# Empty PSUM banks in the tensor engine's order: a NoSync chain on ScalarE and VectorE in a four-layer attention kernel

## The chip, the cores and the metric

The kernel runs on one core of a Trainium2 chip. The core has five engines with an instruction queue each: the tensor engine (PE in the profile, its weight loads PEld), VectorE (DVE), ScalarE (ACT), GpSimd (POOL) and SyncE (SP), which here only starts transfers. The metric is device time in microseconds (us), the median of several runs.

## The reference

Four layers in the order A, B, A, B on x of 2048 x 640 in fp32, each with a layernorm ahead and a residual after: 32 heads of 20. A is linear attention, B is infini attention: causal softmax inside each of four segments of 512 rows, mixed through a gate with a read from a memory that has collected the segments before.

```python
phi = lambda t: jnp.where(t > 0, t + 1, jnp.exp(t))
# A
kv = einsum("bhsd,bhse->bhde", phi(k), v); z = einsum("bhsd->bhd", phi(k))
o = einsum("bhqd,bhde->bhqe", phi(q), kv) / (einsum("bhqd,bhd->bhq", phi(q), z) + 1e-6)
# B, per segment s of 512
a_dot = softmax(qs @ ks.T * scale + causal_mask) @ vs
a_mem = (phi(qs) @ M) / (phi(qs) @ z + 1e-6)
o = g * a_mem + (1 - g) * a_dot
M = M + phi(ks).T @ vs;  z = z + sum(phi(ks))
```

## The kernel before

Products of fp32 matrices are made of two halves in f16 (a high part and the rest), three matmuls for each product. The dense part takes 128 rows or 320 or 512 columns at a time: L325 projects into rows of 320, L311 into a transposed 512, and both leave their result in a bank. PSUM has eight banks of 128 x 512 fp32. Every result of PE goes through one pool of eight, `bank()`; which of the eight a tile gets is settled at build time by the scheduler, from when it expects each to be free.

The program is written as two streams, `dense` (layernorms, transposes, projections, phi, memory, output projections) and `attend` (the softmax attention). `run` alternates between them by a modelled cost, and the order in which it issues matmuls is PE's order as it stands (`MANUAL = ("PE",)`). The order on DVE, ACT, POOL and SP is left to a scheduler, which places an instruction where it expects its inputs.

The attention goes in 64 groups of four heads (eight groups for each of four segments, in two B layers). A group's work is spread over three slots of three stretches (`STRETCHES`):

- row maxes: PE makes scores into two banks (L687, `ks,qs` or `qs,ks`), DVE adds the mask and reduces each with L694, which shows as two rows, the reduction and the read of its accumulator. L703 and L704 split the collected maxes into f16, PE turns them (L712), ACT copies them out (L714), and a transfer puts them as rows under the queries.
- exps: PE makes the scores again, now with the max subtracted (L729), ACT takes the exp out of the bank (L733), POOL sets what the mask hides to zero (L740).
- sums: PE multiplies by the values (L756), ACT copies the bank out (L762).
- normalise: PE turns that (L769), DVE takes the reciprocal of the sums (L772), the gate (L773) and the product out of the bank (L781, or L778 in segment 0), POOL adds to the output (L782).

Beside it the dense stream empties banks too: L272 on ACT copies the high half of a transpose (L268) and L273 on DVE subtracts it to get the rest; phi takes exp (L337) and relu (L339) of a projection; L348 copies the values; L391 adds the residual on DVE; L546 and L547 split queries and keys. A layernorm runs through DVE (L286, L288, L290), POOL (L291), DVE (L293) and ACT (L298).

Of the kernel before, what the change touches and what calls it, by code (L numbers as in the profile page):

```python
# [14 lines left out]
OP = mybir.AluOpType  # L15
# [109 lines left out]
class Kernel:  # L125
    def __init__(self, ctx, tc, A, const, out):
        self.ctx, self.tc, self.nc = ctx, tc, tc.nc
        self.A, self.const, self.out = A, const, out
        pool = lambda name, **k: ctx.enter_context(tc.tile_pool(name=name, bufs=1, **k))
        self.cp = pool("const")  # L130
        self.sb = pool("main")
        self.ps = pool("psum", space=PSUM)
        self.dr = pool("dram", space=DRAM)
        self.rate = 1.0
        self.q_pq, self.q_x, self.q_nat, self.q_row, self.q_w, self.q_pqi = [getattr(self.nc, e) for e in QUEUES]

    def bank(self):
        return self.ps.tile([P, 512], F32, tag="ps", name="ps", bufs=8)
# [122 lines left out]
    def turn(self, src, dst, i):  # L261

        nc = self.nc
        for c0, c1 in ((0, 3), (3, 5)):
            pt = self.bank()
            n = c1 - c0
            for c in range(c0, c1):
                nc.tensor.transpose(pt[:, (c - c0) * P:(c - c0 + 1) * P], src[:, c * P:(c + 1) * P],  # L268
                                    self.ident)
# [63 lines left out]
    def phi(self, p, inv, dst, eps):  # L333
        nc, sb = self.nc, self.sb
        n = p.shape[-1]
        e = sb.tile([P, 512], F32, tag="er", name="e", bufs=3)[:, :n]
        nc.scalar.activation(e, p, AF.Exp, scale=inv)  # L337
        r = sb.tile([P, 512], F32, tag="er", name="r", bufs=3)[:, :n]
        nc.scalar.activation(r, p, AF.Relu, scale=inv)  # L339
        if eps:  # L340
            nc.gpsimd.tensor_scalar(e, e, 1.0, eps, op0=OP.min, op1=OP.add)  # L341
            nc.vector.tensor_tensor(dst, e, r, op=OP.add)
        else:
            nc.vector.scalar_tensor_tensor(dst, e, 1.0, r, op0=OP.min, op1=OP.add)

    def v_half(self, p, v, n):
        vv = v[:, :H * E1].rearrange("p (h e) -> p h e", e=E1)
        self.nc.scalar.activation(vv[:, n * HB:(n + 1) * HB, :DH],  # L348
                                  p.rearrange("p (h e) -> p h e", e=DH), AF.Copy, scale=V_SHIFT)

    def new_v(self, user):

# [6 lines left out]
    def read_mem(self, pq, mem, dst, mul=None):  # L359

        nc, sb = self.nc, self.sb
        cut = HB * E1
        for k in range(2):
            nd = self.bank()
            cost, first = 0, True
            for t in range(C):
                a, b = LO[t] * E1, LO[t] * E1 + WID[t]
                lo, hi = max(a, k * cut), min(b, (k + 1) * cut)
                if lo < hi:
                    nc.tensor.matmul(nd[:, lo - k * cut:hi - k * cut], pq[t],  # L370
                                     mem[:, OFF[t] + lo - a:OFF[t] + hi - a],
                                     start=first, stop=True, skip_group_check=True)
# [4 lines left out]
            nc.vector.tensor_scalar(rc, nd[:, :, DH], 1e-6, None, op0=OP.add)  # L377
            nc.vector.reciprocal(rc, rc)
            if mul is not None:
                nc.vector.tensor_tensor(rc, rc, mul[:, k * HB:(k + 1) * HB], op=OP.mult)  # L380
            nc.vector.tensor_tensor(dst[:, k * HN:(k + 1) * HN].rearrange("p (h e) -> p h e", e=DH),
                                    nd[:, :, :DH], rc[:, :, None].to_broadcast([P, HB, DH]),
                                    op=OP.mult)
            yield cost

    def new_oT(self):
# [1 line left out]

    def o_half(self, oT, wo, L, x, xn, n):
        p = self.proj_n(oT, wo, 0, n)  # L390
        self.nc.vector.scalar_tensor_tensor(xn[:, n * HN:(n + 1) * HN], p, self.io[L],  # L391
                                            x[:, n * HN:(n + 1) * HN], op0=OP.mult, op1=OP.add)


    def norms(self, src, s, box, then=None):
# [21 lines left out]
    def a_first(self, s, xT, w, L, behind=None):  # L417
# [28 lines left out]
        def memory():  # L446
            for b0, b1 in ((0, 3), (3, 5)):
                p = self.bank()
                for i in range(NT):
                    for u in range(b0, b1):  # L450
                        a = OFF[u] - OFF[b0]
                        nc.tensor.matmul(p[:, a:a + WID[u]], pk[i][:, u * P:(u + 1) * P],  # L452
                                         v[i][:, LO[u] * E1:LO[u] * E1 + WID[u]],
                                         start=i == 0 and u == b0, stop=i == NT - 1,
                                         skip_group_check=True)
                a, b = OFF[b0], OFF[b1 - 1] + WID[b1 - 1]
                if s == 0:
                    nc.vector.tensor_copy(acc[:, a:b], p[:, :b - a])
                else:
                    nc.vector.tensor_tensor(acc[:, a:b], p[:, :b - a], acc[:, a:b], op=OP.add)  # L460
                yield (b - a) * 16 * COL
            if s == NSEG - 1:
                L["mem"] = self.masked(acc)
# [78 lines left out]
    def split_store(self, p, dd, t, key):  # L542

        nc = self.nc
        nat = self.bp.tile([P, 2, SEG], F16, tag="nat", name="nat", bufs=2)
        nc.scalar.activation(nat[:, 0], p, AF.Copy, scale=QK_SHIFT)  # L546
# [9 lines left out]
    def b_project(self, st):  # L556
# [14 lines left out]
        def pk_turn():  # L571
# [1 line left out]
            for i in range(NT):  # L573
                nc.tensor.transpose(pt[:, i * P:(i + 1) * P], pkT[:, i * P:(i + 1) * P], self.ident)  # L574
            pk = bp.tile([P, SEG], F32, tag="pkt", name="pkt", bufs=1)
            nc.scalar.activation(pk, pt, AF.Copy)
            return pk

        def update(t, pk):
# [4 lines left out]
                                 start=i == 0, stop=i == NT - 1)  # L584
            a = acc[:, OFF[t]:OFF[t] + WID[t]]
            if s == 0:
                nc.vector.tensor_copy(a, pm[:, :WID[t]])
            else:
                nc.vector.tensor_tensor(a, pm[:, :WID[t]], a, op=OP.add)

        for t in range(C):
            p = yield from self.proj_t(xT, w["q"], t)
# [85 lines left out]
    def row_max(self, G, todo):  # L678
# [11 lines left out]
        for par in range(2):  # L690
            for p, i, a in todo:
                n = (i + 1) * P
                junk = bp.tile([P, SEG], BF16, tag="junk", name="junk", bufs=1)
                nc.vector.tensor_tensor_reduce(junk[:, :n], bs[par][:, a:a + n], self.maskw[:, SEG - n:],  # L694
                                               1.0, NEG, OP.add, OP.max, G["mg"][:, par, p, i:i + 1])
        return cost

    def split_max(self, G):
# [5 lines left out]
        nc.vector.scalar_tensor_tensor(m2[:, :, 1], mg, -1.0 / M_ONE, m2[:, :, 0],  # L704
                                       op0=OP.mult, op1=OP.subtract)
        G["m2"] = m2

    def max_rows(self, G):
# [2 lines left out]
        pt = self.ps.tile([P, 1024], F16, tag="ps", name="pm", bufs=8)  # L711
        nc.tensor.transpose(pt[:32, :P], m2.rearrange("q a k r -> q (a k r)"), self.ident16)  # L712
        mt = bp.tile([32, P], F16, tag="mt", name="mt", bufs=2)
        nc.scalar.activation(mt, pt[:32, :P], AF.Copy)  # L714
# [5 lines left out]
    def scores(self, G, todo):  # L720
# [12 lines left out]
        nc.scalar.activation(e, b, AF.Exp, scale=self.lsc)  # L733
        starts = [a for _, _, _, a in todo]
        if len(starts) == 1:
            d, pat = e[:, :P], [[1, P]]
# [22 lines left out]

    def evacuate(self, G):  # L760
        G["oT"] = self.bp.tile([P, 512], F32, tag="oTf", name="oTf", bufs=1)
        self.nc.scalar.activation(G["oT"], G["pv"], AF.Copy)  # L762

    def normalize(self, G):
        nc, bp, sb, g, st = self.nc, self.bp, self.sb, G["g"], G["st"]
# [2 lines left out]
        for i in range(NT):  # L768
            nc.tensor.transpose(pt[:, i * P:(i + 1) * P], oT[:, i * P:(i + 1) * P], self.ident)  # L769
        pr = pt.rearrange("q (i h e) -> q i h e", i=NT, h=4)  # L770
        rc = sb.tile([P, NT, 4], F32, tag="rc4", name="rc4", bufs=2)
        nc.vector.reciprocal(rc, pr[:, :, :, DH])  # L772
        nc.vector.tensor_tensor(rc, rc, self.gate1[:, None, 4 * g:4 * g + 4].to_broadcast([P, NT, 4]),  # L773
                                op=OP.mult)
        o = st["o"][:, :, 80 * g:80 * g + 80].rearrange("q i (h e) -> q i h e", h=4)
        rb = rc[:, :, :, None].to_broadcast([P, NT, 4, DH])
        if st["s"] == 0:
            nc.vector.tensor_tensor(o, pr[:, :, :, :DH], rb, op=OP.mult)  # L778
        else:
            tmp = sb.tile([P, NT, 4, DH], F32, tag="er", name="tmp", bufs=3)  # L780
            nc.vector.tensor_tensor(tmp, pr[:, :, :, :DH], rb, op=OP.mult)  # L781
# [233 lines left out]
```

## Time and profile before

| | |
|---|---|
| median of three runs | 1830.06 us (1828.65 to 1834.99) |
| profiled execution | 1833.06 us |
| its span | 1831.3 us |
| PE busy | 1713.7 us, 94% |
| DVE busy | 1145.0 us, 63% |
| ACT busy | 911.1 us, 50% |
| POOL busy | 502.5 us, 27% |
| granted PE clock | 0.995 |

A row of a timeline gives the start in the span, the duration, the engine, the line, the operation, output<-inputs, the shape, the count of instructions of one kind drawn together, and in brackets the idle time ahead of it with what ended that. The rows of waits give, for all such idle times of a kind, the sum in us, the count and the mean. A wait for several things is put down to the one that came last.

### The profile page before, as it was taken

The numbers are of one execution on the slowest core, as the hardware profiler recorded it, in microseconds if no ns is written. First come the engines' busy times: TensorE is split into PE (matmuls) and PEld (weight loads), VectorE is DVE, ScalarE is ACT, GpSimd is POOL, SyncE is SP. The second block draws the span as 40 slices with busy tenths as digits, with TensorE's granted clock in tenths as the row PEclk, the third lists the DMA queues.
The fourth block names the chain that finished last, engine by engine and source line by source line (L and its number), as shares of the span: only waits on it lengthen the run. The fifth ranks groups of instructions, "written<-read, shape, count | busy, mean of one in ns | idle before, by whom it ended". The sixth has DMA issues, their size and how long they took to land.

```text
span 1831.3 us, 36161 instructions
## 1 busy us (share of the span) xinstructions
PE 1713.7 (94%) x13032; PEld 1070.3 (58%) x13032; DVE 1145.0 (63%) x3890; ACT 911.1 (50%) x1696; POOL 502.5 (27%) x925
## 2 busy tenths in 40 slices
PE   6999999999999999898989999999999989998998
PEld 4666676654664565453556776766546546544555
DVE  7655343677777676766663421527687777777783
ACT  5455433256556545545554433333664665565553
POOL 1534440022122113224344334200221231232231
PEclk9999999999999999999999999999999999999999
DMA  7452443312222332352212112432122222323332
GB/s 254 154 188 92 159 143 99 107 58 93 88 67 86 105 103 76 105 186 71 66 56 87 51 33 91 137 108 99 51 91 92 86 90 91 101 77 100 122 112 87
DMA packets 123307, 185.96 MB, mean 102 GB/s; under 512 B 13676, under 2 KB 85484, under 8 KB 120952
## 3 DMA queue, kind: packets, MB, share of 16 engines
q1 hardware_dynamic: 109416, 137.44, 23.5%
q0 software_dynamic: 4496, 25.23, 3.8%
q10 hardware_dynamic: 9216, 20.98, 3.0%
q8 instruction: 103, 1.69, 0.4%
q14 instruction: 76, 0.62, 0.1%
HBM read 104.41 MB, written 78.64 MB: 100 GB/s over the span
## 4 chain that ended last, share of the span: by engine, by line
PE 75%; DVE 11%; ACT 6%; issue 4%; POOL 2%; DMA 2%; SPq 1%; POOLq 0%; ACTq 0%; DVEq 0%
PE ps L325 33%; PE ps L311 18%; PE ps L756 7%; DVE junk L694 4%; PE ps L268 4%; ACT pe L733 3%; PE ps L370 3%; PE ps L729 3%; PE ps L452 2%; PE ps L687 2%; POOL e L341 1%; PE ps L582 1%; PE ps L769 1%; DVE nat L547 1%; PE ps L574 1%
## 5 line engine op out<-in xcount | busy, mean ns | idle before, releaser
L694 DVE CUSTOM_DVE_ANT_0 junk<-ps,maskw 128x512 bf16<-128x512 f32 (+3 forms) x1024 | 499.5, 488 | 83.2 <-PE ps L687 27.1
L733 ACT ACTIVATE pe<-ps,lsc 128x512 f32<-128x512 f32 x640 | 392.7, 691 | 174.5 <-PE ps L729 171.5
L740 POOL TENSOR_SCALAR_AFFINE_SELECT pe<-pe 128x256 f32<-128x256 f32 (+1 forms) x640 | 233.5, 371 | 677.4 <-ACT pe L733 672.0
L325 PEld LDWEIGHTS <-xT 128*128 128x128 f16 x2880 | 281.7, 99 | 124.1 <-issue 18.6
L325 PEld LDWEIGHTS <-oT 128*128 128x128 f16 x1920 | 187.1, 98 | 79.6 <-issue 7.6
L341 POOL TENSOR_SCALAR e<-e 128x320 f32<-128x320 f32 (+1 forms) x104 | 163.7, 1574 | 163.2 <-ACT e L337 154.4
L756 PE MATMUL ps<-pe,v 128*32 128x512 f32 (+3 forms) x2048 | 155.4, 438 | 13.7 <-ACT pe L733 6.8
L729 PE MATMUL ps<-qs,ks 62*128 62x384 f16 (+3 forms) x1024 | 132.2, 299 | 33.4 <-DVE mg L694 22.4
L325 PE MATMUL ps<-w_Bo,oT 128*128 128x320 f16 x960 | 142.8, 301 | 2.6 <-DVE mg L694 1.4
L325 PE MATMUL ps<-w_Bv,xT 128*128 128x320 f16 x960 | 141.3, 301 | 1.9 <-DVE mg L694 1.9
L325 PE MATMUL ps<-w_Av,xT 128*128 128x320 f16 x960 | 141.2, 305 | 1.6 <-DVE w_Av L234 1.0
L311 PE MATMUL ps<-xT,w_Bq 128*128 128x512 f16 x600 | 139.5, 379 | 1.5 <-DVE mg L694 0.9
L311 PE MATMUL ps<-xT,w_Bk 128*128 128x512 f16 x600 | 139.5, 379 | 0.2 <-DVE xn L391 0.2
L325 PE MATMUL ps<-w_Ao,oT 128*128 128x320 f16 x960 | 139.5, 299 | 0.0
L311 PE MATMUL ps<-xT,w_Aq 128*128 128x512 f16 x600 | 136.0, 379 | 1.3 <-DVE xT L273 0.9
L325 PE MATMUL ps<-w_Ak,xT 128*128 128x320 f16 x960 | 135.6, 299 | 1.4 <-DVE mg L694 1.4
L348 ACT ACTIVATE v<-ps 128x320 f32<-128x320 f32 x128 | 55.4, 436 | 143.2 <-PE ps L325 138.9
L291 POOL TENSOR_TENSOR rs<-rs,mhalf 128x1 f32<-128x1 f32 x64 | 35.3, 551 | 302.6 <-DVE rs L290 302.6
L687 PE MATMUL ps<-ks,qs 60*128 60x512 f16 (+3 forms) x1024 | 108.4, 297 | 5.8 <-ACT pe L733 3.6
L756 PEld LDWEIGHTS ps<-pe,v 128*32 128x32 f32 x2048 | 65.3, 110 | 81.2 <-issue 66.3
L547 DVE SCALAR_TENSOR_TENSOR nat<-ps,nat 128x512 f16<-128x512 f32 x80 | 55.3, 691 | 90.3 <-ACT nat L546 86.4
L546 ACT ACTIVATE nat<-ps 128x512 f16<-128x512 f32 x80 | 48.0, 600 | 105.9 <-PE ps L311 76.3
(151 smaller groups left out, 2240.9 us busy)
## 6 DMA issues: line engine op xcount, KB each, us to landing
x<-xn ACTq DMA_DIRECT2D x48, 320.0 KB
qs<-qd SPq DMA_DIRECT2D x128, 120.0 KB
ks<-kd SPq DMA_DIRECT2D x128, 120.0 KB
xo<-x SPq DMA_DIRECT2D x48, 320.0 KB
pqd<-pq POOLq DMA_DIRECT2D x40, 256.0 KB, 2.5
pqi<-pqd SPq DMA_DIRECT2D x32, 320.0 KB
qd<-nat SPq DMA_DIRECT2D x40, 256.0 KB
kd<-nat SPq DMA_DIRECT2D x40, 256.0 KB
```

Of the source, the lines that this page charges most:

```text
L268: nc.tensor.transpose(pt[:, (c - c0) * P:(c - c0 + 1) * P], src[:, c * P:(c + 1) * P], self.ident)
L311: nc.tensor.matmul(p, w[:, c, a, t * P:(t + 1) * P], xT[:, c, b, :], start=k == 0, stop=k == 3 * C - 1)
L325: nc.tensor.matmul(p, xT[:, c, a, i * P:(i + 1) * P], w[:, c, b, n * HN:(n + 1) * HN], start=k == 0, stop=k == 3 * C - 1)
L341: nc.gpsimd.tensor_scalar(e, e, 1.0, eps, op0=OP.min, op1=OP.add)
L348: self.nc.scalar.activation(vv[:, n * HB:(n + 1) * HB, :DH], p.rearrange("p (h e) -> p h e", e=DH), AF.Copy, scale=V_SHIFT)
L547: nc.vector.scalar_tensor_tensor(nat[:, 1], p, QK_SHIFT, nat[:, 0], op0=OP.mult, op1=OP.subtract)
L687: nc.tensor.matmul(bs[par][:, a:a + n], qs[r, p, i * P:(i + 1) * P], ks[r, p, :n], start=True, stop=True)
L694: nc.vector.tensor_tensor_reduce(junk[:, :n], bs[par][:, a:a + n], self.maskw[:, SEG - n:], 1.0, NEG, OP.add, OP.max, G["mg"][:, par, p, i ...
L729: nc.tensor.matmul(b[:, a:a + n], ks[r, p, j * P:(j + 1) * P], qs[r, p, j * P:], start=True, stop=True)
L733: nc.scalar.activation(e, b, AF.Exp, scale=self.lsc)
L740: nc.gpsimd.affine_select(d, d, pattern=pat, compare_op=OP.is_ge, fill=0.0, base=0, channel_multiplier=-1)
L756: nc.tensor.matmul(G["pv"][32 * h4:32 * h4 + 32, j * P:], v[j][:, h * E1:h * E1 + 32], G.pop((p, par, j)), start=j == 0, stop=j == 2, skip ...
```

## The change

Every instruction on ACT and DVE that is the first to empty a bank, and the two that split the maxes, goes through a new `seq`. It ties the instruction to the one that went through `seq` before it on the same engine, by a dependency without a semaphore: nothing waits at run time for it, but the scheduler may no longer swap the two. Since the program is written in PE's order, the tied instructions of an engine now issue in the order in which PE fills their banks. Instructions that aren't tied (L273, L547, the layernorm's, all on POOL and SP) are still placed by the scheduler, between the tied ones.

The tied lines are L272, L337, L339, L348, L546, L576, L714, L733, L762 on ACT, and L377 to L381, L391, L458, L460, L587, L589, L694, L703, L704, L772, L773, L778, L781 on DVE. The core of the diff; the other lines are wrapped in the same way:

```diff
+        self.last = {}
+    def seq(self, ins):
+        i = ins.ins
+        prev = self.last.get(i.engine)
+        if prev is not None:
+            self.tc.add_manual_dep(i, prev.name, mybir.DependencyInfo(mybir.DependencyClass.NoSync,
+                                                                      mybir.DependencyReason.DATA), reason="seq")
+        self.last[i.engine] = i
...
-            nc.scalar.activation(hi, v, AF.Copy)
+            self.seq(nc.scalar.activation(hi, v, AF.Copy))
             nc.vector.tensor_tensor(dst[:, c0:c1, 1, i * P:(i + 1) * P], v, hi, op=OP.subtract)
...
-        nc.scalar.activation(e, p, AF.Exp, scale=inv)
+        self.seq(nc.scalar.activation(e, p, AF.Exp, scale=inv))
...
-        nc.scalar.activation(r, p, AF.Relu, scale=inv)
+        self.seq(nc.scalar.activation(r, p, AF.Relu, scale=inv))
...
-                nc.vector.tensor_tensor_reduce(junk[:, :n], bs[par][:, a:a + n], self.maskw[:, SEG - n:],
-                                               1.0, NEG, OP.add, OP.max, G["mg"][:, par, p, i:i + 1])
+                self.seq(nc.vector.tensor_tensor_reduce(junk[:, :n], bs[par][:, a:a + n], self.maskw[:, SEG - n:],
+                                                        1.0, NEG, OP.add, OP.max, G["mg"][:, par, p, i:i + 1]))
...
-        nc.vector.tensor_scalar(m2[:, :, 0], mg, -1.0 / M_ONE, None, op0=OP.mult)
+        self.seq(nc.vector.tensor_scalar(m2[:, :, 0], mg, -1.0 / M_ONE, None, op0=OP.mult))
...
-        nc.scalar.activation(e, b, AF.Exp, scale=self.lsc)
+        self.seq(nc.scalar.activation(e, b, AF.Exp, scale=self.lsc))
...
-        nc.vector.reciprocal(rc, pr[:, :, :, DH])
+        self.seq(nc.vector.reciprocal(rc, pr[:, :, :, DH]))
```

The build moves rows on both engines and leaves PE's as they were. In the rows that follow, the lines of the changed kernel stand 11 further down than in the kernel before (L694 is L705 there). A name with a number is one tile: `ps_` a bank, `mg_` the maxes of a group.

On DVE, where a group is normalised (the bank `ps_6354`) while the next group's row maxes come in (`ps_6365`, `ps_6366`), the kernel before has

```order
L273 TENSOR_TENSOR xT_5526<-ps_6332,xT_5526 128x2x128
L772 RECIPROCAL rc4_6359<-ps_6354 128x16
L694 ISA junk_6369,mg_6213<-ps_6365,maskw_76 128x512
L694 ISA mg_6213 128x1
L773 TENSOR_TENSOR rc4_6359<-rc4_6359,gate1_2322 128x16
L694 ISA junk_6371,mg_6213<-ps_6366,maskw_76 128x512
L694 ISA mg_6213 128x1
L781 TENSOR_TENSOR tmp_6362<-ps_6354,rc4_6359 128x320
```

and the changed kernel has

```order
L284 TENSOR_TENSOR xT_5526<-ps_6332,xT_5526 128x2x128
L783 RECIPROCAL rc4_6359<-ps_6354 128x16
L784 TENSOR_TENSOR rc4_6359<-rc4_6359,gate1_2322 128x16
L792 TENSOR_TENSOR tmp_6362<-ps_6354,rc4_6359 128x320
L705 ISA junk_6369,mg_6213<-ps_6365,maskw_76 128x512
L705 ISA mg_6213 128x1
L705 ISA junk_6371,mg_6213<-ps_6366,maskw_76 128x512
L705 ISA mg_6213 128x1
```

The three links of the normalise stand together now, ahead of both maxes; before, each link had a max behind it.

On ACT, where phi of the queries (`e_4765` and `r_4767`, out of `ps_4696`) meets two exps of scores (`pe_4773`, `pe_4779`), before:

```order
L546 ACTIVATE nat_4759<-ps_4696 128x512
L733 ACTIVATE pe_4773<-ps_4770,lsc_2314 128x512
L733 ACTIVATE pe_4779<-ps_4776,lsc_2314 128x512
L337 ACTIVATE e_4765<-ps_4696,inv_Bq_1789 128x512
L339 ACTIVATE r_4767<-ps_4696,inv_Bq_1789 128x512
L714 ACTIVATE mt_4806<-pm_4804 32x128
```

and after:

```order
L557 ACTIVATE nat_4759<-ps_4696 128x512
L348 ACTIVATE e_4765<-ps_4696,inv_Bq_1789 128x512
L350 ACTIVATE r_4767<-ps_4696,inv_Bq_1789 128x512
L744 ACTIVATE pe_4773<-ps_4770,lsc_2314 128x512
L744 ACTIVATE pe_4779<-ps_4776,lsc_2314 128x512
L725 ACTIVATE mt_4806<-pm_4804 32x128
```

The phi has moved ahead of the two exps, since PE filled its bank first.

On DVE, where a layernorm (`rs_3901`, `nb_3904`) and the residual adds of the layer's end (`xn_3910`) meet a group's row maxes, before:

```order
L290 TENSOR_SCALAR rs_3901<-mv_3899 128x1
L694 ISA junk_3949,mg_3793<-ps_3945,maskw_76 128x512
L694 ISA mg_3793 128x1
L293 TENSOR_SCALAR nb_3904<-mv_3899,rs_3901 128x1
L694 ISA junk_3951,mg_3793<-ps_3946,maskw_76 128x512
L694 ISA mg_3793 128x1
L694 ISA junk_3959,mg_3793<-ps_3953,maskw_76 128x384
L694 ISA mg_3793 128x1
L694 ISA junk_3961,mg_3793<-ps_3953,maskw_76 128x128
```

and, with five more rows of maxes between:

```order
L391 SCALAR_TENSOR_TENSOR xn_3910<-ps_3911,ioA_2168,xo_3908 128x320
L391 SCALAR_TENSOR_TENSOR xn_3910<-ps_3928,ioA_2168,xo_3908 128x320
L273 TENSOR_TENSOR xT_3555<-ps_3988,xT_3555 128x3x128
```

and after:

```order
L301 TENSOR_SCALAR rs_3901<-mv_3899 128x1
L304 TENSOR_SCALAR nb_3904<-mv_3899,rs_3901 128x1
L402 SCALAR_TENSOR_TENSOR xn_3910<-ps_3911,ioA_2168,xo_3908 128x320
L402 SCALAR_TENSOR_TENSOR xn_3910<-ps_3928,ioA_2168,xo_3908 128x320
L705 ISA junk_3949,mg_3793<-ps_3945,maskw_76 128x512
L705 ISA mg_3793 128x1
L284 TENSOR_TENSOR xT_3555<-ps_3988,xT_3555 128x3x128
L705 ISA junk_3951,mg_3793<-ps_3946,maskw_76 128x512
L705 ISA mg_3793 128x1
L284 TENSOR_TENSOR xT_3555<-ps_3994,xT_3555 128x2x128
L705 ISA junk_3959,mg_3793<-ps_3953,maskw_76 128x384
L705 ISA mg_3793 128x1
```

The adds stood behind all of the group's maxes, and stand ahead of the first now; L273 (L284 there), which isn't tied, comes between the maxes, and L293 (L304 there) with no max between it and L290.

More of the change, by code (lines that the diff above doesn't have):

```diff
@@ L390, in o_half @@
         p = self.proj_n(oT, wo, 0, n)
-        self.nc.vector.scalar_tensor_tensor(xn[:, n * HN:(n + 1) * HN], p, self.io[L],
-                                            x[:, n * HN:(n + 1) * HN], op0=OP.mult, op1=OP.add)
+        self.seq(self.nc.vector.scalar_tensor_tensor(xn[:, n * HN:(n + 1) * HN], p, self.io[L],
+                                                     x[:, n * HN:(n + 1) * HN], op0=OP.mult, op1=OP.add))
     def norms(self, src, s, box, then=None):
@@ L457, in memory @@
                 if s == 0:
-                    nc.vector.tensor_copy(acc[:, a:b], p[:, :b - a])
+                    self.seq(nc.vector.tensor_copy(acc[:, a:b], p[:, :b - a]))
                 else:
-                    nc.vector.tensor_tensor(acc[:, a:b], p[:, :b - a], acc[:, a:b], op=OP.add)
+                    self.seq(nc.vector.tensor_tensor(acc[:, a:b], p[:, :b - a], acc[:, a:b], op=OP.add))
                 yield (b - a) * 16 * COL
@@ L575, in pk_turn @@
             pk = bp.tile([P, SEG], F32, tag="pkt", name="pkt", bufs=1)
[L576 removed]
+            self.seq(nc.scalar.activation(pk, pt, AF.Copy))
             return pk
@@ L586, in update @@
             if s == 0:
-                nc.vector.tensor_copy(a, pm[:, :WID[t]])
+                self.seq(nc.vector.tensor_copy(a, pm[:, :WID[t]]))
             else:
-                nc.vector.tensor_tensor(a, pm[:, :WID[t]], a, op=OP.add)
+                self.seq(nc.vector.tensor_tensor(a, pm[:, :WID[t]], a, op=OP.add))
         for t in range(C):
```

34 lines of the change are left out of this document (17 added, 17 removed).

## The prediction

> **What bounds the kernel now.** I read the page first (span, busy time, the chain of waits by engine), then busy time by stretches, then the waits of the tensor engine, and last the timelines of single places.
>
> ```profile
> span 1831.3 us, 36161 instructions
> PE 1713.7 (94%) x13032; PEld 1070.3 (58%) x13032; DVE 1145.0 (63%) x3890; ACT 911.1 (50%) x1696; POOL 502.5 (27%) x925
> PE 75%; DVE 11%; ACT 6%; issue 4%; POOL 2%; DMA 2%; SPq 1%; POOLq 0%; ACTq 0%; DVEq 0%
> ```
>
> PE is the bound: it is busy for 1713.7 of 1831.3 us, so 117.6 us are all that an order of other engines could win. The profiled execution took 1833.06 us, 1.8 more than its span and 3.0 more than the median of the three runs, 1830.06. I sum against 1833.06 and carry the difference over to the median. The runs spread from 1828.65 to 1834.99; what a measurement of this kernel can tell from no change is about 0.3%, 5.5 us.
>
> Where PE idles, by stretches (start:end, length, then busy us of PE, PEld, DVE, ACT and POOL):
>
> ```profile
> 0.00:137.00 137.00, 118.23 (x753) 80.65 (x754) 90.35 (x215) 69.49 (x126) 48.77 (x64) 0.99 0.55 198
> 503.00:686.00 183.00, 172.90 (x1411) 107.51 (x1409) 133.79 (x480) 95.31 (x178) 38.42 (x95) 1.00 0.28 91
> 960.00:1098.00 138.00, 137.71 (x982) 97.92 (x980) 44.30 (x113) 56.71 (x114) 50.75 (x52) 1.00 0.17 57
> ```
>
> The opening loses 18.8 us to loads and first steps, and a stretch of the A layer 0.3. The remainder lies in the attention of the B layers: 10.1 us of the middle stretch's 183. There PE waits for banks of PSUM that DVE or ACT has yet to empty (waiting tile, releaser: us, count, mean):
>
> ```profile
> PE ps L729 <- DVE mg L694: 22.4, 42, 1.0
> PE ps L268 <- DVE mg L694: 7.1, 15, 0.5
> PE ps L756 <- ACT pe L733: 6.8, 17, 0.7
> PE pm L712 <- DVE m L704: 6.0, 9, 1.2
> PE ps L325 <- DVE mg L694: 5.2, 10, 1.0
> ```
>
> So 22.4 + 7.1 + 5.2 = 34.7 us wait for the row maxes of L694, of which each reads a bank of scores. PE's own order is written by hand and its rows are the same in both kernels. What can change is which instruction empties which bank when, and which bank a tile is handed: about a third of the 2372 PSUM tiles get another bank.
>
> **The change, part by part.** It adds no instruction, it only turns the order on DVE and ACT. On DVE 185 blocks move, on ACT 30. I laid both orders on the trace of before and looked at each place where the tile's new bank comes free later, or a wait goes.
>
> *The normalise on DVE* (56 of 64 are moved). Before, its three links alternate with row maxes; now L772, L773, L781 stand together, the maxes behind. A typical place, DVE first, then PE:
>
> ```profile
> 536.81 0.26 DVE L772 RECIPROCAL rc<-ps 128x16 f32<-128x16 f32 x1 [1.52 <-PE ps L769]
> 537.13 0.69 DVE L694 CUSTOM_DVE_ANT_0 junk<-ps,maskw 128x512 bf16<-128x512 f32 x1
> 537.75 0.08 DVE L694 DVE_READ_ACCUMULATOR2_ANT mg<- 128x1 f32 x1
> 537.75 0.17 DVE L773 TENSOR_TENSOR rc<-rc,gate 128x16 f32<-128x16 f32 x1
> 537.97 0.69 DVE L694 CUSTOM_DVE_ANT_0 junk<-ps,maskw 128x512 bf16<-128x512 f32 x1
> 538.59 0.08 DVE L694 DVE_READ_ACCUMULATOR2_ANT mg<- 128x1 f32 x1
> 538.59 0.48 DVE L781 TENSOR_TENSOR tmp<-ps,rc 128x320 f32<-128x320 f32 x1
> ```
>
> ```profile
> 537.15 1.10 PE L729 MATMUL ps<-qs,ks 62*128 62x512 f16 x4
> 538.73 0.55 PE L268 MATMUL ps<-ident,xh 128*128 128x128 f32 x3 [0.47 <-DVE mg L694]
> 539.11 2.20 PE L325 MATMUL ps<-w_Bv,xT 128*128 128x320 f16 x15
> ```
>
> The fourth score tile (the last of the four at 537.15) starts at 537.88, when the first max has ended at 537.83. The next tile, L268, waits 0.47 us for the second max, ended at 538.67. What the three links cost back to back is seen at a place that isn't moved:
>
> ```profile
> 975.67 0.26 DVE L772 RECIPROCAL rc<-ps 128x16 f32<-128x16 f32 x1 [1.40 <-PE ps L769]
> 975.96 0.17 DVE L773 TENSOR_TENSOR rc<-rc,gate 128x16 f32<-128x16 f32 x1
> 976.17 0.49 DVE L781 TENSOR_TENSOR tmp<-ps,rc 128x320 f32<-128x320 f32 x1
> ```
>
> From the start of L772 to the end of L781 it is 976.66 - 975.67 = 0.99 us. In the new order the normalise's bank is thus free at 536.81 + 0.99 = 537.80. The build hands that bank to the fourth score tile, so its start stays at 537.88. The first max now begins at about 537.72 (an independent instruction starts some 0.08 ahead of its predecessor's end, as L781 does at 538.59 beside the read that ends at 538.67) and ends, 0.70 later, at 538.42. L268 takes that bank and starts at 538.47 rather than 538.73: 0.26 us won. The next, L325, takes an exp's bank, free by then. Such a second wait stands at 35 of the moved places (15 at L268, 10 at L729, 8 at L325, 2 at L311): 35 x 0.26 = **9.1 us won**. DVE ends the set about 0.3 us later; in this stretch it is busy 133.79 of 183 us, which covers that. Without cover it would be 56 x 0.3 = 17 us.
>
> [...]
>
> *Earlier tails.* At four places the residual add (L391) and the layernorm's L298 come earlier in the row, so that the exp behind them does; at two, L704 comes ahead of a max:
>
> ```profile
> 524.37 0.38 PE L687 MATMUL ps<-ks,qs 60*128 60x256 f16 x3 [0.51 <-ACT pe L733]
> 529.48 0.23 PE L712 MATMUL pm<-ident,m 128*32 128x128 f16 x1 [1.24 <-DVE m L704]
> ```
>
> The first kind wins up to its 0.51 each, four times 2.0, less 0.2 each where a BN instruction now delays L773: 1.2. The second moves past one max of 0.70: 1.4. Together **2.6 won**.
>
> *The bank of the weighted sums* (seven places). On ACT phi's pair L337, L339 now issues ahead of two exps. The bank of L756 was that of the first exp; it becomes that of a row max:
>
> ```profile
> 424.79 1.31 ACT L733 ACTIVATE pe<-ps,lsc 128x512 f32<-128x512 f32 x2
> 425.67 2.36 PE L756 MATMUL ps<-pe,v 128*32 128x512 f32 x32 [0.21 <-ACT pe L733]
> 427.96 0.66 PE L574 MATMUL ps<-ident,pkT 128*128 128x128 f32 x4
> 426.32 0.08 DVE L694 DVE_READ_ACCUMULATOR2_ANT mg<- 128x1 f32 x1
> ```
>
> The max ends at 426.40, so L756 starts at 426.46 rather than 425.67: 0.79 here, 0.5 to 0.8 at the others; 7 x 0.67 = **4.7 lost**. The exps come 1.4 us later, but the sums read them in the last third of their 2.36 us.
>
> *The second score bank behind a phi* (seven places). It comes no more from L781 but from phi's L339:
>
> ```profile
> 595.16 0.49 DVE L781 TENSOR_TENSOR tmp<-ps,rc 128x320 f32<-128x320 f32 x1
> 595.23 0.68 ACT L339 ACTIVATE r<-ps,inv_Bq 128x512 f32<-128x512 f32 x1
> 595.29 0.80 PE L729 MATMUL ps<-qs,ks 62*128 62x512 f16 x2 [0.91 <-DVE mg L694]
> ```
>
> L781 ends at 595.65, and L339 at 595.91: 7 x 0.27 = **1.9 lost**.
>
> *A new wait at the head of DVE's queue* (two places, here and one layer pair later). The layernorm's L293 waits for POOL's L291. Before, a max stood ahead of it and the two residual adds behind all maxes; now L290, L293, L391, L391 come first, and every following max stands behind an L273 that waits for ACT.
>
> ```profile
> 370.30 0.55 POOL L291 TENSOR_TENSOR rs<-rs,mhalf 128x1 f32<-128x1 f32 x1 [7.93 <-DVE rs L290]
> 371.01 0.37 PE L729 MATMUL ps<-qs,ks 62*128 62x512 f16 x1 [0.35 <-DVE mg L694]
> 371.85 0.37 PE L729 MATMUL ps<-qs,ks 62*128 62x512 f16 x1 [0.47 <-DVE mg L694]
> 372.01 2.40 ACT L733 ACTIVATE pe<-ps,lsc 128x512 f32<-128x512 f32 x4
> 372.74 0.77 PE L268 MATMUL ps<-ident,xh 128*128 128x128 f32 x5 [0.51 <-ACT pe L733]
> ```
>
> L293 can't start before 370.85. Queued behind it are the adds and all row maxes of the group, and PE's next tiles wait for those banks. The build hands the two score tiles the banks of the four exps instead, which end 0.6 apart from 372.7 on: the first starts at 372.74 (1.73 later), the second at 373.3 (1.5 later). Lost is 1.5 if the row catches up behind it, 2.3 if the late maxes hold one more tile; I take 1.9: 2 x 1.9 = **3.8 lost**.
>
> *Nine smaller places* where a bank-emptying instruction now stands behind one that waits. The trace of before cannot show them; the nearest row is that of the sums, 0.79 each, and the other bound nothing, since a later wait can absorb the shift. Half: 9 x 0.39 = **3.5 lost** (0 to 7.1).
>
> **Sum.** Won 9.1 + 2.6 = 11.7; lost 4.7 + 1.9 + 3.8 + 3.5 = 13.9; net 2.2 us slower. On the profiled execution that is 1835.3, on the median 1830.06 + 2.2 = **1832.3 us**. Its own range: with half of the normalise's gain given back (4.5 lost more) the small places at nothing or in full (3.5 either way) and the new heads at 1.5 to 2.3 (0.8 either way), 1828 to 1841.
>
> **Rivals.**
>
> *Gains only.* The losses lie in front of waits that exist anyway: L756 waits 17 times, 6.8 us, and a later start may only shorten the next wait. For it: PE has 10.1 us of slack in 183. Against it: behind L756 at 425.67 the next tile (L574 at 427.96) has no wait that a shift could shorten. It gives 1830.06 - 11.7 = 1818.4.
>
> *Full rotation.* Emptying in the order in which PE asks removes all waits for the row maxes: 34.7 us, 1795.4. Against it: the fourth score bank above does not start a moment earlier, since both orders free a bank at 537.8. [...]
>
> *Chaining is free.* If dependent links followed as closely as independent ones, two links would start 0.11 sooner each and the maxes 0.22: 35 x 0.22 = 7.7 more, 1824.6. The row at 975.67 speaks against it.
>
> *Head of line, slower.* The order by PE's need puts instructions of far-apart streams in one row; one that isn't ready holds all behind it. The place is L293 behind POOL's L291 (and L273 behind ACT), ahead of row maxes; the price is the 1.9 of above; it decides from two further places on (2.2 + 3.8 = 6.0). I found two from before's times, but with shifted times more arise; eight more of the layernorms would give 2.2 + 15.2, so 1847.5. For it: DVE is busy 73% there and its row now leaves no choice. Against it: 42 L729 waits show that PE is itself often late. [...]
>
> *Nothing of it.* The moved rows lie in idle time of DVE and ACT (37% and 50% of the span): 1830.
>
> **Chances.** Forecast 0.40 (0.28 of it inside 5.5 us, 0.12 slower), gains only 0.22, full rotation 0.05, free chaining 0.05 (0.03 faster, 0.02 inside), head of line 0.20, nothing 0.08. So faster 0.22 + 0.05 + 0.03 = 0.30, same 0.28 + 0.08 + 0.02 = 0.38, slower 0.12 + 0.20 = 0.32. Cases of both signs hold most, so the range reaches from gains only to eight more heads, 1816 to 1847; full rotation and the far tail are left out.
>
> **What would show it.** Right: L268's wait for L694 falls to about half (7.1 to some 3 us); L756 waits for DVE's L694 at seven places; L729 at 371 waits for ACT's L733 by over 1.5 us; POOL's L291 becomes a releaser of DVE. Wrong: the first L694 behind a grouped normalise ends over 1.7 us after L772's start (no gain), waits for L694 fall below 15 us (rotation), or waits behind L293 or L273 appear at more than four places (head of line).

## The result and the profile after

The changed kernel takes 1871.58 us (median of four runs, 1869.77 to 1879.44) against 1829.42 beside it: a ratio of 1.0225 with a 95% interval of 1.0208 to 1.0243, so 41 to 42 us slower. The forecast was 1832.3 in a range that ended at 1847. The profiled execution's span is 1867.9 us, 36.6 longer than before's.

The page after, span and busy time:

```profile
span 1867.9 us, 36139 instructions
PE 1730.8 (93%) x13032; PEld 1079.1 (58%) x13032; DVE 1168.6 (63%) x3890; ACT 913.3 (49%) x1696; POOL 500.0 (27%) x925
```

PE's idle time has grown from 117.6 to 137.1 us, and PE and DVE are busy longer with the same number of instructions: PE by 17.1 us, DVE by 23.6. A good half of PE's 17.1 us is the granted clock, 0.995 in the profiled execution before and 0.990 in the one after: (1 - 0.990) x 1867.9 = 18.7 us of PE's full clock are lost, against (1 - 0.995) x 1831.3 = 9.2. From 300 us on, the trace after has eleven stretches of 3.41 us at a granted clock of 0.50 where the one before has four; each loses half its length, so 7 x 1.71 = 12 us are the clock's there.

The waits of PE after (waiting tile, releaser: us, count, longest; the third figure is the longest wait in the rows of before too, and not the mean, but no sum of the forecast uses it):

```profile
PE ps L740 <- DVE tmp L792: 14.8, 26, 1.6
PE ps L767 <- DVE mg L705: 6.7, 7, 1.2
PE ps L740 <- ACT pe L744: 6.4, 7, 2.1
PE ps L740 <- DVE otok L789: 5.4, 10, 0.9
PE ps L698 <- DVE oa L392: 4.2, 4, 1.0
PE ps L740 <- DVE otok L392: 4.0, 5, 0.8
PE ps L740 <- DVE mg L705: 3.8, 13, 0.7
PE ps L279 <- DVE mg L705: 3.3, 15, 0.2
PE ps L336 <- DVE mg L705: 1.7, 8, 0.2
```

Of the 34.7 us of waits for the row maxes in the forecast's three rows 8.8 are left (3.8 + 3.3 + 1.7), and others stand in their place: for the normalise (L792, and L789 in segment 0), for the memory read's division (L392), for an exp (L744). Since PE runs the same 13032 instructions in the same order in both traces, but for a few neighbouring rows, I took for each the start after minus the start before. Where that difference grows, time is lost; where it shrinks, it is won. By places, in us of the traces:

| place | forecast | measured |
|---|---|---|
| second wait behind a normalise, 33 of 35 found | 9.1 won | 8.0 won |
| earlier tails (near 524, 692, 1429, 1578) | 2.6 won | 1.9 won |
| bank of the weighted sums, 7 | 4.7 lost | 9.3 lost |
| score bank behind phi, 7 | 1.9 lost | 1.6 lost |
| head of DVE's queue near 370 and 1274 | 3.8 lost | 6.4 lost |
| "nine smaller places": all else from 300 us on | 3.5 lost | about 32 lost |

Of the clock's 12 us, 1.7 lie in the row of the heads, near 370, and some 10 in the last row.

The normalise is as forecast, PE first and then DVE (the place shown of before at 536.81):

```profile
546.05 1.09 PE L740 MATMUL ps<-qs,ks 62*128 62x512 f16 x4
547.36 0.55 PE L279 MATMUL ps<-ident,xh 128*128 128x128 f32 x3 [0.22 <-DVE mg L705]
547.74 1.52 PE L336 MATMUL ps<-w_Bv,xT 128*128 128x320 f16 x10
```

```profile
545.71 0.26 DVE L783 RECIPROCAL rc<-ps 128x16 f32<-128x16 f32 x1 [1.52 <-PE ps L780]
546.00 0.17 DVE L784 TENSOR_TENSOR rc<-rc,gate 128x16 f32<-128x16 f32 x1
546.21 0.49 DVE L792 TENSOR_TENSOR tmp<-ps,rc 128x320 f32<-128x320 f32 x1
546.62 0.68 DVE L705 CUSTOM_DVE_ANT_0 junk<-ps,maskw 128x512 bf16<-128x512 f32 x1
547.22 0.08 DVE L705 DVE_READ_ACCUMULATOR2_ANT mg<- 128x1 f32 x1
```

The first max ends at 547.30, 1.59 us after L783's start, and L279 waits 0.22 where it had waited 0.47. What makes up the other rows of the table is read below, with the runs that tell it apart.

### The profile page after: what moved, and what is told of

Read it like the earlier page. It is cut to its first block, busy times and chain, and to the rows that moved or that the text cites. A ratio compares the mean times of both kernels' runs of the same rounds, so it can differ in the third digit from the quotient of the medians.

```text
span 1867.9 us, 36139 instructions
## 1 busy us (share of the span) xinstructions
PE 1730.8 (93%) x13032; PEld 1079.1 (58%) x13032; DVE 1168.6 (63%) x3890; ACT 913.3 (49%) x1696; POOL 500.0 (27%) x925
## 5 line engine op out<-in xcount | busy, mean ns | idle before, releaser
L705 DVE CUSTOM_DVE_ANT_0 junk<-ps,maskw 128x512 bf16<-128x512 f32 (+3 forms) x1024 | 500.4, 489 | 79.9 <-PE ps L698 12.0
L744 ACT ACTIVATE pe<-ps,lsc 128x512 f32<-128x512 f32 x640 | 392.4, 690 | 180.9 <-PE ps L740 178.6
L336 PEld LDWEIGHTS <-xT 128*128 128x128 f16 x2880 | 282.1, 99 | 118.2 <-issue 12.1
L336 PEld LDWEIGHTS <-oT 128*128 128x128 f16 x1920 | 187.2, 98 | 79.5 <-issue 7.5
L767 PE MATMUL ps<-pe,v 128*32 128x512 f32 (+3 forms) x2048 | 159.1, 442 | 15.7 <-DVE mg L705 6.7
L336 PE MATMUL ps<-w_Bo,oT 128*128 128x320 f16 x960 | 142.8, 301 | 2.0 <-ACT oT L283 0.6
L336 PE MATMUL ps<-w_Bv,xT 128*128 128x320 f16 x960 | 142.7, 303 | 0.9 <-DVE mg L705 0.9
L336 PE MATMUL ps<-w_Av,xT 128*128 128x320 f16 x960 | 139.4, 302 | 1.3 <-DVE w_Av L245 1.0
L322 PE MATMUL ps<-xT,w_Bq 128*128 128x512 f16 x600 | 139.5, 379 | 1.1 <-DVE acc L600 0.4
L322 PE MATMUL ps<-xT,w_Bk 128*128 128x512 f16 x600 | 139.5, 379 | 0.4 <-ACT pe L744 0.4
L336 PE MATMUL ps<-w_Ao,oT 128*128 128x320 f16 x960 | 139.8, 299 | 0.0
L336 PE MATMUL ps<-w_Ak,xT 128*128 128x320 f16 x960 | 137.1, 301 | 0.2 <-DVE mg L705 0.2
L322 PE MATMUL ps<-xT,w_Aq 128*128 128x512 f16 x600 | 136.0, 379 | 0.3 <-ACT xT L283 0.3
L698 PE MATMUL ps<-ks,qs 60*128 60x512 f16 (+3 forms) x1024 | 112.0, 298 | 14.7 <-DVE oa L392 4.2
L359 ACT ACTIVATE v<-ps 128x320 f32<-128x320 f32 x128 | 55.4, 435 | 140.1 <-PE ps L336 136.7
L767 PEld LDWEIGHTS ps<-pe,v 128*32 128x32 f32 x2048 | 66.5, 110 | 87.0 <-issue 76.5
L558 DVE SCALAR_TENSOR_TENSOR nat<-ps,nat 128x512 f16<-128x512 f32 x80 | 55.2, 691 | 86.0 <-ACT nat L557 83.9
L740 PEld LDWEIGHTS <-ks 62*128 62x128 f16 x1024 | 40.1, 94 | 110.2 <-issue 41.9
```

What stands on the lines that cost most here:

```text
L322: nc.tensor.matmul(p, w[:, c, a, t * P:(t + 1) * P], xT[:, c, b, :], start=k == 0, stop=k == 3 * C - 1)
L336: nc.tensor.matmul(p, xT[:, c, a, i * P:(i + 1) * P], w[:, c, b, n * HN:(n + 1) * HN], start=k == 0, stop=k == 3 * C - 1)
L359: self.seq(self.nc.scalar.activation(vv[:, n * HB:(n + 1) * HB, :DH], p.rearrange("p (h e) -> p h e", e=DH), AF.Copy, scale=V_SHIFT))
L698: nc.tensor.matmul(bs[par][:, a:a + n], qs[r, p, i * P:(i + 1) * P], ks[r, p, :n], start=True, stop=True)
L705: self.seq(nc.vector.tensor_tensor_reduce(junk[:, :n], bs[par][:, a:a + n], self.maskw[:, SEG - n:], 1.0, NEG, OP.add, OP.max, G["mg"][:, ...
L740: nc.tensor.matmul(b[:, a:a + n], ks[r, p, j * P:(j + 1) * P], qs[r, p, j * P:], start=True, stop=True)
```

## The experiments

All kernels keep the change's code and give `seq` a kind; only kinds in `TIED` are tied. The last ones also fix the banks by a table. The kinds are, on ACT, oh (L283), phi (L348, L350), v (L359), nat (L557), pk (L587), row (L725), exp (L744), copy (L773), and on DVE, ao (the division, L388 to L392), res (L402), acc, upd (memory sums), max (L705), m2 (L714, L715), norm (L783 to L792), all by the changed kernel's lines.

```diff
-    def seq(self, ins):
+    def seq(self, kind, ins):
+        if kind not in TIED:
+            return
...
-        self.seq(nc.scalar.activation(e, p, AF.Exp, scale=inv))
+        self.seq('phi', nc.scalar.activation(e, p, AF.Exp, scale=inv))
```

**VectorE alone, ScalarE alone.** Theory 1 is the sum of places, theory 2 blames the banks that tiles are handed.

```diff
+TIED = ('ao', 'res', 'acc', 'upd', 'max', 'm2', 'norm')
```

> Only VectorE's bank-emptying instructions are tied; ScalarE's are left to the scheduler. Theory 1 (the loss is a sum of places: on ScalarE phi ahead of the exps, about 9.3 us at the sums' bank and 1.6 at the score bank behind phi; the rest on VectorE): 1829 + 42 - 11 = 1860. Theory 2 (the loss comes from the other PSUM banks that tiles are handed, whatever the queue order): the banks differ from before's in 607 of 2372 tiles here and in 672 with all tied, so 1867 or so. Theory 3 (the two orders need each other: either alone is harmless): 1830.

Measured: 1856.43 against 1832.44, ratio 1.0122 (1.0104 to 1.0140).

```diff
+TIED = ('oh', 'phi', 'v', 'nat', 'pk', 'row', 'exp', 'copy')
```

> Only ScalarE's are tied. Theory 1: 1829 + 11 = 1840, and only the places of the weighted sums and of the score bank behind phi are late. Theory 2: 122 tiles have another bank, a fifth of the change's, so 1837. Theory 3: 1830.

Measured: 1850.41, ratio 1.0094 (1.0063 to 1.0125). The two add up to 2.16% of the change's 2.25%: each engine's ties cost by themselves, so theory 3 falls. ScalarE's share was larger than theory 1 had it, 18 us and not 11, and VectorE's smaller, 24 and not 31. Theory 2 fits badly: with ScalarE alone 122 tiles have another bank, of the 672 with all tied, and that cost 0.94 of the 2.25%. The sums' bank is lost with ScalarE alone, as the place shows in its trace (the line numbers there stand one further than in the changed kernel):

```profile
427.78 2.87 PE L768 MATMUL ps<-pe,v 128*32 128x512 f32 x32 [1.10 <-DVE mg L706]
```

and not with VectorE alone:

```profile
427.85 2.36 PE L768 MATMUL ps<-pe,v 128*32 128x512 f32 x32 [0.21 <-ACT pe L745]
```

**The attention's own on VectorE, and all but the tails.**

```diff
+TIED = ('max', 'm2', 'norm')
```

> Only the attention's own on VectorE are tied to each other: row maxes, their split, and the normalise (L705, L714, L715, L783 to L792 by the changed kernel's lines). Theory 1: the gain of 0.24 at 33 places comes without the losses: 1829 - 8 = 1821. A rival on VectorE's time (grouped dependent links no longer overlap with others, and the changed kernel's VectorE is busy 23.6 us longer): about half of these links are the normalise's, so VectorE is some 12 us busier here and the kernel no faster, 1829 to 1837.

Measured: 1832.70, ratio 1.0002 (0.9992 to 1.0012). Theory 1 missed: the gain of 0.24 a place is there (L280 below waits 0.22 at the place of 538.73 of before), but as much is given back at other places (score bank behind phi 1.6, L687 behind L273 1.5, three more at the sums' bank 1.1, the last part of the run 2.4, of which 1.7 are the clock). The rival's time, 1829 to 1837, came, but not its reason in full: DVE is busy for 1151.1 us here, 6 longer than before and not 12.

```profile
539.08 0.55 PE L280 MATMUL ps<-ident,xh 128*128 128x128 f32 x3 [0.22 <-DVE mg L706]
```

```diff
+TIED = ('oh', 'phi', 'v', 'acc', 'nat', 'pk', 'upd', 'max', 'm2', 'row', 'exp', 'copy', 'norm')
```

> All tied but the memory read's division (L388 to L392) and the residual add (L402). Theory 1: the places at which these stand among row maxes (the two layer heads 6.4, the tails 4.3, the four L392 places 5.8, 1.8 and the late stretch near 1690 with 7.1, less 1.9 won) go: 1871.6 - 23.5 = 1848. If the losses lie with the row maxes and the normalise: 1868 or more.

Measured: 1851.21, ratio 1.0100 (1.0082 to 1.0119). The division and the residual add carry 20 us.

**Each of the two, and all but phi and both.**

```diff
+TIED = ('oh', 'phi', 'v', 'res', 'acc', 'nat', 'pk', 'upd', 'max', 'm2', 'row', 'exp', 'copy', 'norm')
```

> All tied but the memory read's division (L388 to L392); the residual add stays tied. Untying both won 20 us. If the division carries it (by the places: tails 2.9, L392 places 5.8, 1.8, the late stretch 7.0): 1854. If the residual add does: 1868. The two layer heads near 370 and 1275 should stay late (6.4) if they are the residual add's, and go if not.

Measured without the division: 1860.98, ratio 1.0159 (1.0140 to 1.0177); 10.6 us of the change's 1871.58 go. The heads stay, 7.8 us late in this trace (3.4 of it the clock), and the tails near 451, the L392 places and the late stretch near 1690 are at 1.4, 0.0 and 0.1.

```diff
+TIED = ('oh', 'phi', 'v', 'ao', 'acc', 'nat', 'pk', 'upd', 'max', 'm2', 'row', 'exp', 'copy', 'norm')
```

> All tied but the residual add (L402). If the two layer heads are its own: 6.4 won plus what it holds up in the late stretch near 1690, 1862; if the division carries all: 1871.

Measured without the residual add: 1861.81, ratio 1.0164 (1.0148 to 1.0181); 9.8 us go, and the heads with them (0.0 late near 370, and near 1275 no difference but the clock's), while the L392 places (4.5) and the late stretch (5.1, of it 1.7 the clock) stay.

```diff
+TIED = ('oh', 'v', 'acc', 'nat', 'pk', 'upd', 'max', 'm2', 'row', 'exp', 'copy', 'norm')
```

> All tied but the three kinds that the places point to: phi, the division and the residual add. If these three carry the loss: no slower than the run with the attention's own on VectorE alone, 1833. If the many small ties together cost something: above 1838.

Measured: 1833.08, ratio 1.0003 (0.9994 to 1.0013). So phi's tie is worth 18.1 us (1851.21 to 1833.08), the division's 10.6, the residual add's 9.8, and the twelve other kinds together, with these three untied, nothing that can be told from zero. These are differences between kernels measured at different times; by the ratios, each against before beside it, they are 17.8, 12.1 and 11.2 us, to within some 4 us each.

DVE's busy time tells where its own 23.6 us come from. With the division untied, and with the residual add untied:

```profile
PE 1733.0 (93%) x13032; PEld 1076.3 (58%) x13032; DVE 1152.4 (62%) x3890; ACT 911.6 (49%) x1696; POOL 499.8 (27%) x925
```

```profile
PE 1727.8 (93%) x13032; PEld 1076.9 (58%) x13032; DVE 1167.2 (63%) x3890; ACT 911.7 (49%) x1696; POOL 499.8 (27%) x925
```

Some 16 of the 23.6 us are the division's links, most of the rest (6) the normalise's.

**Order against banks.** Here the bank of each of the 2372 tiles comes from a table, with eight tags of one buffer for one tag of eight.

```diff
-        return self.ps.tile([P, 512], F32, tag="ps", name="ps", bufs=8)
+        return self.ps.tile([P, 512], F32, tag=self.tag(), name="ps", bufs=1)
+
+    def tag(self):
+        self.nps = getattr(self, "nps", -1) + 1
+        return "ps" + BANKS[self.nps]
```

All tied, the banks of before:

```diff
+TIED = ('oh', 'phi', 'v', 'ao', 'res', 'acc', 'nat', 'pk', 'upd', 'max', 'm2', 'row', 'exp', 'copy', 'norm')
+BANKS = (
...
```

> All instructions tied as in the changed kernel, but every PSUM tile is given, by a table, the bank that it had before the change. If the other banks were what cost time, and not the order on the queues: 1830. If the order costs and the banks follow from it: no better than the change, 1872; worse if the old banks don't fit the new order (by the changed kernel's trace, 127 us of tiles would start ahead of their bank's release; with half absorbed 1930).

Measured: 1920.61, ratio 1.0479 (1.0463 to 1.0494). Theory 2 falls: the old banks don't bring the old time back, and the build's new ones were its answer to the new order. How much the order costs by itself isn't shown by this run, since the old banks were chosen for the other order.

All tied, the banks fitted to the changed kernel's trace:

```diff
+TIED = ('oh', 'phi', 'v', 'ao', 'res', 'acc', 'nat', 'pk', 'upd', 'max', 'm2', 'row', 'exp', 'copy', 'norm')
+BANKS = (
...
```

> All tied as in the changed kernel, the banks exchanged by the changed kernel's trace (75 exchanges, waits 91 to 70 us). If the order itself holds the banks late: 1872 - 21 = 1851, still slower than before by 19; if the build's poor choice of banks is all of the loss: 1830 or less.

Measured: 1861.25, ratio 1.0159 (1.0138 to 1.0180). These banks win 10 of the change's 42 us, where 21 were expected; that a better table could win more isn't ruled out.

Nothing tied, the banks fitted to before's trace:

```diff
+TIED = ()
+BANKS = (
...
```

> Nothing tied, the order on all queues that of before (two rows differ); the table of banks is made from the trace of before: where a tile would wait and another bank was free earlier, it takes that (62 exchanges). The waits for banks add up to 71 us by that trace and to 49 with the exchanges: 22 less if later waits don't take it back, 1810; if the waits are set by the lack of any free bank, 1832.

Measured with before's order, but for two rows of DVE: 1816.19, ratio 0.9908 (0.9892 to 0.9925), 16 of the 22 us. With banks fitted once to each, the new order is thus 45 us slower than the old (1861.25 against 1816.19), as much as with the build's banks: as far as one fit of each can show, it is the order that costs.

The attention's own on VectorE tied, the banks fitted to its trace:

```diff
+TIED = ('max', 'm2', 'norm')
+BANKS = (
...
```

> Row maxes, split and normalise tied as in the run of that part alone, and the banks exchanged by its trace (66 exchanges, waits 68 to 53 us): 1832.5 - 15 = 1817. If what the ties win is the same as what the exchanges win (both give the second tile an earlier bank), it is no better than the exchanges alone, 1810 to 1817; if they add, 1802.

Measured: 1824.91, ratio 0.9953 (0.9938 to 0.9968). With banks fitted once to each, tying the attention's own on VectorE is a loss of 8.7 us (1824.91 - 1816.19), which no part of the expectation had.

Nothing tied, the banks fitted a second time:

```diff
+TIED = ()
+BANKS = (
...
```

> Nothing tied; the banks fitted once more, to the trace of the kernel with fitted banks (7 more exchanges, waits 52.7 to 50.3 us by it): 1816.2 - 2 = 1814, or 1816 if what is left are places without any free bank.

Measured: 1814.35, ratio 0.9905 (0.9888 to 0.9922): no more than the first fit can be claimed, and both beat the two kernels of the study. How that comes about is seen at the place of 536 to 539 in the trace with fitted banks (L284 there is L268):

```profile
534.64 1.10 PE L745 MATMUL ps<-qs,ks 62*128 62x512 f16 x4
535.80 0.55 PE L284 MATMUL ps<-ident,xh 128*128 128x128 f32 x3
536.22 2.20 PE L341 MATMUL ps<-w_Bv,xT 128*128 128x320 f16 x15
```

L284 has no wait at all, though each link of the normalise still has a max behind it. Before, L268 had been handed the bank of the second max, and L325, which starts 0.38 later, that of an exp that had ended 0.86 us earlier; the two needed only to be exchanged.

## Why the prediction was wrong

**Right: the bound, and the gain.** PE and its waits for banks are what moved, though PE's busy time, which the forecast left as it was, moved too. The normalise's chain took what its unmoved row said (0.99 us there, 546.70 - 545.71 = 0.99 here) and won 0.24 a place against 0.26 forecast. L756 waits for a row max at seven places, as said. "Full rotation" fell, though the sign set for it (below 15 us) came on the forecast's three rows with 8.8; with L767's 6.7 and 1.3 at L698 and L322 the waits for row maxes are 16.8. The others only changed their releaser, so the sum over all releasers should have been the sign. POOL's L291 as a releaser of DVE was no sign either, since it ended 45 waits (20.3 us) before and 48 (23.8 us) after. "Free chaining" fell with L792's 0.99.

**The step that failed** is "nine smaller places ... the nearest row is that of the sums, 0.79 each". The row was put at 3.5 us and measured about 32. There were more than nine places, and several cost 1 to 7 us; the runs show that the ties of phi, the division and the residual add carry nearly all of the loss. Some 10 of the 32 us are PE's clock, a term that the forecast put at nothing without a reason: it took PE's 1713.7 busy us as fixed, and 117.6 us as all that an order can move. The list came from laying the new queue on the old times and asking which tile's new bank comes free late. That finds the first tile of a place, but not what the engine's own row does once it is made serial, since those times were taken from the old order. The forecast looked for banks; most of the time went in queues. The rival head of line, at 0.20, came nearest, and even its 1847.5 was too low. What it says, that one instruction that isn't ready holds all behind it, is seen at phi and at the residual add (waits of 0.88 and 2.38 us, in the rows below), and its sign came: L698 waits behind L284 seven times, 2.6 us, where L687 had waited behind L273 twice, 0.3 us. At the division the traces show another thing, links that wait for each other (0.03 us from the end of one to the start of the next, in the rows that follow).

*The division* was not in the forecast at all. In the last memory reads four divisions come in a row. The changed kernel's DVE runs them link after link; the last one, then the normalise:

```profile
1711.95 0.17 DVE L388 TENSOR_SCALAR rc<-ps 128x16 f32<-128x16 f32 x1
1712.15 0.25 DVE L389 RECIPROCAL rc<-rc 128x16 f32<-128x16 f32 x1
1712.43 0.18 DVE L391 TENSOR_TENSOR rc<-rc,gate 128x16 f32<-128x16 f32 x1
1712.64 0.49 DVE L392 TENSOR_TENSOR otok<-ps,rc 128x320 f32<-128x320 f32 x1
1713.05 0.25 DVE L783 RECIPROCAL rc<-ps 128x16 f32<-128x16 f32 x1
```

A division takes 1713.05 - 1711.95 = 1.10 us. Before, the scheduler put the links of different divisions between each other, so that each covered the next one's start:

```profile
1681.05 0.43 DVE L381 TENSOR_TENSOR otok<-ps,rc 128x320 f32<-128x320 f32 x1
1681.39 0.16 DVE L380 TENSOR_TENSOR rc<-rc,gate 128x16 f32<-128x16 f32 x1
1681.47 0.17 DVE L377 TENSOR_SCALAR rc<-ps 128x16 f32<-128x16 f32 x1
1681.59 0.49 DVE L381 TENSOR_TENSOR otok<-ps,rc 128x320 f32<-128x320 f32 x1
1681.99 0.24 DVE L378 RECIPROCAL rc<-rc 128x16 f32<-128x16 f32 x1
1682.15 0.19 DVE L772 RECIPROCAL rc<-ps 128x16 f32<-128x16 f32 x1
```

Here L381, L380, L377, L381, L378, 1.49 us of instructions, take 1682.15 - 1681.05 = 1.10. PE pays for the difference where it comes back for a bank:

```profile
1712.09 0.49 PE L740 MATMUL ps<-qs,ks 62*128 62x512 f16 x2 [0.72 <-DVE otok L392]
1713.31 0.37 PE L740 MATMUL ps<-qs,ks 62*128 62x512 f16 x1 [0.73 <-DVE rc L783]
```

Before, those two waits together were the 0.58 of one:

```profile
1683.11 0.61 PE L729 MATMUL ps<-qs,ks 62*128 62x512 f16 x2 [0.58 <-DVE mg L694]
```

The forecast had "in this stretch it is busy 133.79 of 183 us, which covers that". It said so of the normalise alone, where the run of the attention's own found no loss (1832.70). A mean over a stretch covers nothing at the point where four divisions, a normalise and six maxes come at once. "Without cover it would be 56 x 0.3 = 17 us" stood there too, and was not put into the range. That the division's 10.6 us come from its serial links everywhere is argued from such rows, not tested.

*The sums' bank* was the right mechanism at half its size. The rows at the first place, ACT, then PE, then POOL:

```profile
427.42 0.69 ACT L348 ACTIVATE e<-ps,inv_Bq 128x512 f32<-128x512 f32 x1 [0.88 <-DVE nat L558]
428.01 0.68 ACT L350 ACTIVATE r<-ps,inv_Bq 128x512 f32<-128x512 f32 x1
428.58 1.27 ACT L744 ACTIVATE pe<-ps,lsc 128x512 f32<-128x512 f32 x2
```

```profile
428.14 2.87 PE L767 MATMUL ps<-pe,v 128*32 128x512 f32 x32 [1.09 <-DVE mg L705]
```

```profile
429.33 0.41 POOL L751 TENSOR_SCALAR_AFFINE_SELECT pe<-pe 128x256 f32<-128x256 f32 x1 [2.81 <-ACT pe L744]
429.92 0.41 POOL L751 TENSOR_SCALAR_AFFINE_SELECT pe<-pe 128x256 f32<-128x256 f32 x1 [0.18 <-ACT pe L744]
```

The wait is 0.88 longer, as forecast (0.79). But phi's exp waits 0.88 us for DVE's L558, a wait that two exps had covered before, and holds them behind it. They start at 428.58, 2.2 us later by PE's time there and not 1.4, so that the masked exps come too late for the last third of the sums: L767 lasts 2.87 us where it lasted 2.36. That 0.5 was the forecast's "but the sums read them in the last third", a cover that was gone. Phi costs at other places too (near 466 and 1371, 3.0 us with ScalarE alone and without the clock, at L698 behind L350).

*The layer's head* was found, and priced at 1.9. The two places lost 4.2 and 2.2 us, and 1.7 of the first are the clock, so the price was near. The first, DVE, then PE:

```profile
368.37 0.21 DVE L304 TENSOR_SCALAR nb<-mv,rs 128x1 f32<-128x1 f32 x1 [0.73 <-POOL rs L302]
369.41 0.68 DVE L705 CUSTOM_DVE_ANT_0 junk<-ps,maskw 128x512 bf16<-128x512 f32 x1
372.49 0.56 DVE L284 TENSOR_TENSOR xT<-ps,xT 128x384 f16<-128x384 f32 x1 [2.38 <-ACT xT L283]
372.96 0.68 DVE L705 CUSTOM_DVE_ANT_0 junk<-ps,maskw 128x512 bf16<-128x512 f32 x1
```

```profile
370.22 0.37 PE L740 MATMUL ps<-qs,ks 62*128 62x512 f16 x1 [2.08 <-ACT pe L744]
371.38 1.02 PE L279 MATMUL ps<-ident,xh 128*128 128x128 f32 x5 [0.21 <-ACT pe L744]
372.23 3.88 PE L336 MATMUL ps<-w_Bv,xT 128*128 128x320 f16 x15
```

PE waits 2.08 for the exp's bank, 1.73 more than before, exactly the forecast's step. Then the untied L284 waits 2.38 us for ACT's copy of L279's tile, and the second max stands behind it with its bank. The rest of the excess at this place is in the last row: the 15 matmuls of L336 take 3.88 us where they took 2.20, which is the clock (0.50 granted, below).

Phi, the division and the residual add carry 38.5 of the change's 42 us by the runs that untied them (18.1 + 10.6 + 9.8). How much of phi's 18.1 is the sums' bank and how much is spread is read from the traces only (8.4 of 16.6 us in the run with ScalarE alone). Nor is the clock told apart from the ties: the granted clock was 0.985 to 0.990 with all tied, 0.990 to 0.993 without the division and the residual add, and 0.993 to 0.996 without phi too, so it falls where PE waits more, and no run here moves one without the other.

## What to carry to other kernels

An order that was right for the consumer of the buffers was not right here for the engines that empty them (41 to 42 us slower): a tie that looks free, since it has no semaphore, takes away the scheduler's choice to put independent instructions between dependent ones, and lets one that isn't ready hold those behind it, as L284's 2.38 us near 370 held a row max. Price such a change by running each queue forward in its new order, not by laying the new order on old times, count the places by kind before giving the leftover a price, and leave room for PE's clock, which took some 10 of the 36.6 us of trace here. And where a tensor engine waits for a bank, ask first whether another bank was free: 62 exchanges of banks won 0.9% with the queues as they were but for two rows.

## What the runs showed of the hardware

**Stretches of 3.41 us at half the granted clock stood behind patchy work of PE.** The windows around the head near 370 in the changed kernel (start:end, length, busy of PE, PEld, DVE, ACT, POOL, then the granted clock):

```profile
366.00:372.50 6.50, 3.98 (x28) 1.96 (x26) 3.39 (x16) 3.77 (x7) 1.72 (x5) 0.98 0.25 78
372.50:375.70 3.20, 3.20 (x14) 1.82 (x13) 3.20 (x11) 0.32 (x1) 0.00 (x0) 0.50 0.27 102
```

PE was busy 3.98 of 6.50 us, its longest wait 2.08 and its gaps 2.5 in all, and the matmuls that follow ran at a granted clock of 0.50: of 3.20 us 1.6 are lost. Before, the same place (idle 1.33 us in three pieces) ran at a clock of 1.00, but such a stretch came at 819, 938, 1276 and 1717 of that trace. It came after short waits too: near 891 in the changed kernel those ahead of it are 0.80, 0.53 and 0.21 us.

```profile
887.69:891.10 3.41, 1.86 (x13) 0.98 (x11) 3.05 (x10) 2.55 (x4) 2.28 (x6) 1.00 0.20 77
891.10:894.52 3.42, 3.42 (x22) 1.58 (x19) 1.57 (x8) 1.19 (x3) 0.18 (x1) 0.50 0.02 5
```

Ahead of each such place from 300 us on, in both traces and but for the run's end, PE had been busy for 0.63 to 2.28 of 3.41 us. It did not come behind every such patch: from 508.01 to 511.42 in the changed kernel PE was busy for 1.56 of 3.41 us, and the granted clock of the next 3.41 us was 1.00. So near 370 the wait of 2.08 us was followed by a loss of 1.6 more, and waits of 1.04 and 0.80 near 510 by none; what sets a stretch off isn't shown by these runs.

**VectorE overlapped independent instructions by 0.05 to 0.09 us.** In the rows near 1681, an instruction that needs nothing of its predecessor starts 0.05 to 0.09 us ahead of its end; in the rows near 546 and 1712, a link of a normalise or of a division that takes its predecessor's result starts 0.03 to 0.04 behind it. Over 3890 instructions the changed order cost 23.6 us of busy time.
